# One more expert by seven products, a second buffer pair for the weight sums, and work moved from VectorE to ScalarE in a fused attention, MoE and MLP kernel

## The chip, the cores and the metric

The kernel runs as one program on one core of a Trainium2 chip. A core has TensorE (PE in the rows, its weight loads PEld), VectorE (DVE), ScalarE (ACT), GpSimd (POOL) and SyncE (SP, which here only issues DMAs). The metric is the device time of one execution in microseconds. Everything is float32 at the edges; inside, a float32 operand is split into a rounded high part (type fp32r) and the rest, and one product is made from three TensorE products: high by high, high by rest, rest by high.

## The reference

Three layers follow each other: attention that keeps the 32 largest scores of each row, a mixture of eight experts whose gates are balanced over all tokens, and an MLP with the Mish function whose weights come as float64.

```python
scores = scale * np.matmul(q, k.transpose(0, 1, 3, 2))      # 2 x 8 heads, 576 x 576, head 64
kth = np.partition(scores, -top_k, axis=-1)[..., -top_k:-top_k + 1]
attn = np.matmul(softmax(np.where(scores >= kth, scores, -1e9)), v)
...
P = np.exp(logits - logits.max())                            # 1152 tokens x 8 experts
for _ in range(8):
    P /= P.sum(1, keepdims=True) + 1e-09
    P /= P.sum(0, keepdims=True) + 1e-09
    P *= N / E
for e in range(E):
    out += P[:, e:e + 1] * (np.maximum(x @ w1[e], 0.0) @ w2[e])   # 512 -> 1024 -> 512
...
h = x @ w_in                                                 # 512 -> 2048
return (h * np.tanh(log1p(exp(h)))) @ w_out                  # 2048 -> 512
```

## The kernel before, in words

The 1152 tokens are nine tiles of 128 rows, in three chunks: tiles 0 and 1, tiles 2 and 3, tiles 4 to 8. While VectorE still searches the attention of later tiles for their 32 largest scores, TensorE already runs the experts on the chunks whose attention is done. The gates need all tokens, so the expert outputs of the first two chunks ("spilled" rows, 32 blocks of 128 x 512) go to DRAM as they are. The third chunk (tag c2) starts when attention has ended; from then on its outputs, and the spilled ones that are read back, are multiplied by the gate and added into one accumulator `acc` for each tile. Last comes the MLP in two passes, d0 over tiles 0 to 3 and d1 over tiles 4 to 8.

Weights come in pieces of 128 hidden columns: 128 x 512 of the first layer and 128 x 512 of the second, eight pieces for an expert. In a **plain** piece (`ffn_pass`) the two halves are fetched (`wraw0`, `wraw1`), ScalarE rounds each to its high part (`wh`, line 535), GpSimd or VectorE subtracts for the rest (`wl`, line 536), TensorE makes the first layer (`h`, line 787, 24 products over 640 token columns), ScalarE the high part of the ReLU (`hh`, line 618), VectorE the rest (`hl`, line 619), and two pieces later TensorE the second layer (`y`, line 664, 15 products of 512 columns for five tiles).

In a **pair** (`pair_pass`) two pieces are taken together as a 2 x 2 block product by seven products instead of eight (line 696), each of six TensorE instructions. The seven left sides are made from the two raw weight halves `ra` and `rb` in `load_pair`: the blocks 11 and 12 as they are, the sums s1 to s4 by four GpSimd instructions (lines 557 to 560), and 22. Rounding and subtracting then give `wh` and `wl` of four groups, named 11 (11 and 12), s2 (s2 and s3), s1 (s1 and 22) and s4. The right sides t1 to t4 are sums of token blocks: GpSimd makes those of chunk c2, VectorE those of d0 and d1 (`steps`, lines 595 to 605; "lefts" in the code). TensorE's order in a pair is 11, 12, s2, s3, s1, 22, s4; between them stand the second layers of earlier pieces in halves ("carried", two tiles early, the others late). ScalarE copies partial sums out of PSUM: `p1`, `u2`, `u3` (line 708); VectorE adds them to later ones (`c`, line 714). The bank that holds s3's sum is written again by product 22, so TensorE can go on there only when `u3` is out.

The raw tiles of `ra` and `rb` share three buffers (`wraw0`), each group of `wh` and `wl` has one of four. Experts 0 to 6 of chunk c2 are plain (`PLAIN = 7`), expert 7, d0 and d1 go in pairs.

Beside the products of chunk c2 two other streams are dealt out piece by piece (`pace`): the 32 spilled rows, read back and combined by VectorE (`combine`, lines 806 and 808, 128 x 512 each), and the 32 conversions of the float64 MLP weights (`double_to_float`, lines 929 to 944): a DMA of both words (`cx`), the square of the upper word by ScalarE (`cd`, line 935), six VectorE instructions (lines 936, 939 to 943), a DMA to DRAM. `pace` allows the row n - 10 and the conversion 0.74 (n - 11) + 1 to begin after VectorE's `hl` of piece n. Finished tiles of `acc` are turned by TensorE (`x2t`, line 967, in the PSUM bank "misc" that the pairs also use for product 12) to become the MLP's input.

Engines run their instructions in the order in which a scheduler has put them, TensorE's in the order of the code; each waits at the head of its queue for semaphores. `after(a, b)` puts a behind b in the order without a semaphore.

## Time and profile before

| | us |
|---|---|
| device time, median of 3 runs | 1205.79 |
| lowest and highest of the 3 | 1204.71, 1210.03 |
| the profiled execution | 1205.91 |
| its span, first to last instruction | 1204.1 |
| TensorE busy in the span | 1153.7 |
| VectorE busy | 939.9 |
| ScalarE busy | 695.9 |
| GpSimd busy | 661.0 |

The span is the stretch that the trace covers; the profiled execution took 1.8 us more than it. Attention and the first two chunks take the time to about 556 us, the last product of chunk c2 ends at about 1009, the first of d1 starts at about 1090. In the rows, a group is "line engine operation out<-in, partitions x elements", its count, its busy time and mean, and after the second bar how long the engine stood idle before it and for whom.

### The profile page before, as it was taken

To read this page: it belongs to the slowest core of one execution; us is meant where nothing else is said; L and a number is where in the kernel's file an instruction comes from. 1 tells how busy PE (TensorE), PEld (TensorE's weight loads), DVE (VectorE), ACT (ScalarE), POOL (GpSimd) and SP (SyncE) were. 2 spreads that over 40 slices of the span, in tenths; PEclk is the share of its full clock that TensorE was granted. 3 is DMA by queue.
4 is the path that set the end of the run, shared out by engine and by line. 5 is a ranking of instruction groups with operands and counts; after the bars stand their busy time and mean duration, and the time that the engine had idled before them with its cause. 6 is when DMAs were issued, how large, how long until landed. Compare 5 with 4: busy or idle time off the path is not lost.

```text
span 1204.1 us, 21260 instructions
## 1 busy us (share of the span) xinstructions
PE 1153.7 (96%) x7299; PEld 1028.0 (85%) x7299; DVE 939.9 (78%) x1975; ACT 695.9 (58%) x1414; POOL 661.0 (55%) x559
## 2 busy tenths in 40 slices
PE   3778999999999999999999999999999999999998
PEld 2566888998988899898999989989999998888997
DVE  7999999999999999923666888888767556686442
ACT  5877777777778777754223333333343347666653
POOL 6545877878787777752123243333212466777561
PEclk9999999999999999999999999999999999999999
DMA  8357555557565455544225556656543222223211
GB/s 252 115 181 253 182 182 182 178 174 232 168 215 161 160 167 164 185 141 140 88 85 187 184 193 195 206 184 212 175 155 108 77 73 88 97 97 114 91 51 44
DMA packets 105836, 184.68 MB, mean 153 GB/s; under 512 B 14208, under 2 KB 24704, under 8 KB 105728
## 3 DMA queue, kind: packets, MB, share of 16 engines
q1 hardware_dynamic: 104432, 182.15, 47.2%
q8 instruction: 57, 0.93, 0.3%
q10 hardware_dynamic: 1296, 1.18, 0.3%
q14 instruction: 51, 0.42, 0.1%
HBM read 159.43 MB, written 23.86 MB: 152 GB/s over the span
## 4 chain that ended last, share of the span: by engine, by line
PE 82%; DVE 5%; POOL 3%; DMA 2%; ACT 2%; issue 1%; POOLq 0%; DVEq 0%; ACTq 0%; SPq 0%
PE y_c2e L664 17%; PE h_c2e L787 15%; PE h_c1e L787 8%; PE y_c1e L664 8%; PE y_d L664 6%; PE y_c0e L664 6%; PE h_c0e L787 6%; PE h_d L696 5%; PE pv L356 2%; PE tr L333 2%; PE sc L234 2%; PE h_c2e L696 2%; DVE top L262 1%; PE pv L363 1%; DVE w L269 1%
## 5 line engine op out<-in xcount | busy, mean ns | idle before, releaser
L536 POOL TENSOR_TENSOR wl_c2e<-wraw_c2e,wh_c2e 128x512 fp32r<-128x512 f32 x56 | 75.5, 1348 | 261.9 <-ACT wh_c2e L535 261.9
L536 POOL TENSOR_TENSOR wl_c1e<-wraw_c1e,wh_c1e 128x512 fp32r<-128x512 f32 x128 | 171.7, 1353 | 59.8 <-ACT wh_c1e L535 57.4
L536 POOL TENSOR_TENSOR wl_c0e<-wraw_c0e,wh_c0e 128x512 fp32r<-128x512 f32 x112 | 148.3, 1336 | 49.3 <-ACT wh_c0e L535 43.7
L262 DVE MAX8 top<-w 128x8 f32<-128x576 f32 x216 | 158.4, 748 | 1.0
L535 ACT ACTIVATE wh_c2e<-wraw_c2e 128x512 fp32r<-128x512 f32 x112 | 70.6, 631 | 149.0 <-PE y_c2e L664 67.3
L787 PE MATMUL h_c2e<-xh,wh_c2e 128*128 128x256 f32 x448 | 138.2, 308 | 1.3 <-DVE hl_c2e L619 1.3
L787 PE MATMUL h_c2e<-xl,wh_c2e 128*128 128x256 f32 x448 | 137.4, 307 | 0.0
L787 PE MATMUL h_c2e<-xh,wl_c2e 128*128 128x256 f32 x448 | 137.4, 307 | 0.0
L619 DVE SCALAR_TENSOR_TENSOR hl_c2e<-h_c2e,hh_c2e 128x256 fp32r<-128x256 f32 (+1 forms) x116 | 56.4, 486 | 69.0 <-ACT hh_c2e L618 68.7
L664 PE MATMUL y_c2e<-wh_c2e,hl_c2e 128*128 128x512 f32 x280 | 110.2, 394 | 0.0
L664 PE MATMUL y_c2e<-wh_c2e,hh_c2e 128*128 128x512 f32 x280 | 110.0, 393 | 0.0
L664 PE MATMUL y_c2e<-wl_c2e,hh_c2e 128*128 128x512 f32 x280 | 109.6, 392 | 0.0
L535 ACT ACTIVATE wh_c1e<-wraw_c1e 128x512 fp32r<-128x512 f32 x128 | 80.5, 629 | 47.1 <-PE y_c1e L664 22.1
L269 DVE MATCH_REPLACE8 w<-top,w 128x576 f32<-128x576 f32 x144 | 106.5, 740 | 0.0
L535 ACT ACTIVATE wh_c0e<-wraw_c0e 128x512 fp32r<-128x512 f32 x112 | 70.3, 629 | 43.9 <-PE y_c0e L664 17.6
L787 PEld LDWEIGHTS h_c2e<-xh,wh_c2e 128*128 128x128 f32 x448 | 84.2, 188 | 4.3 <-DVE hl_c2e L619 2.3
L234 PE MATMUL sc<-ks,q 128*128 128x288 f32 x320 | 65.5, 336 | 23.1 <-POOL ks L166 6.1
L787 PEld LDWEIGHTS h_c2e<-xl,wh_c2e 128*128 128x128 f32 x448 | 84.3, 188 | 2.0
L787 PEld LDWEIGHTS h_c2e<-xh,wl_c2e 128*128 128x128 f32 x448 | 84.2, 188 | 0.0
L234 PEld LDWEIGHTS sc<-ks,q 128*128 128x128 f32 x320 | 52.7, 209 | 33.7 <-POOL ks L166 9.9
L787 PE MATMUL h_c1e<-xh,wh_c1e 128*128 128x256 f32 (+1 forms) x256 | 76.4, 298 | 0.0
L787 PE MATMUL h_c1e<-xh,wl_c1e 128*128 128x256 f32 (+1 forms) x256 | 73.3, 286 | 0.0
(540 smaller groups left out, 3622.8 us busy)
## 6 DMA issues: line engine op xcount, KB each, us to landing
wraw_c1e<-in_wst_dram SPq DMA_DIRECT2D x128, 256.0 KB, 2.9
wraw_c0e<-in_wst_dram SPq DMA_DIRECT2D x112, 256.0 KB, 3.0
wraw_c2e<-in_wst_dram SPq DMA_DIRECT2D x112, 256.0 KB, 3.1
cx<-in_w_dram SPq DMA_DIRECT2D x32, 512.0 KB, 3.9
yd<-ysp SPq DMA_DIRECT2D x32, 256.0 KB, 3.6
yb<-yd SPq DMA_DIRECT2D x32, 256.0 KB, 3.4
w<-cb SPq DMA_DIRECT2D x32, 256.0 KB, 3.3
kraw<-in_kT_dram SPq DMA_DIRECT2D x17, 288.0 KB, 3.0
```

The lines of the kernel that those rows point to most:

```text
L234: nc.tensor.matmul(halves[half], q[:, h % HG, :], ks[b, h][:, half * HS : (half + 1) * HS], start=(i == 0), stop=(i == len(terms) - 1),)
L262: top8 = nc.vector.max(g, src)
L269: nc.vector.match_replace(w, g, src, NEG)
L333: nc.tensor.transpose(tr[:, c, :], em[:, j * D + c * P :][:, :P], ident)
L356: nc.tensor.matmul(pv[i * D : (i + 1) * D, pair, c0:c1], vmain[b, pair][:, i, c, :], live["at", i][:, c, c0:c1], start=(c == 0), stop=False,)
L363: nc.tensor.matmul(pv[:, pair, c0:c1], vtail[b, pair], at2[:, c0:c1], start=False, stop=True)
L535: nc.scalar.activation(hi, raw, AF.Copy)
L536: eng.tensor_sub(lo, raw, hi)
L619: live["hl"] = nc.vector.scalar_tensor_tensor(l, ps, 0.0, h, op0=ALU.max, op1=ALU.subtract)
L664: nc.tensor.matmul(y, h[:, j * P : (j + 1) * P], w, start=(start and k == 0), stop=(stop and k == len(products) - 1))
L696: nc.tensor.matmul(bank, a[:, cols], b[:, c, :], start=(start and c + k == 0), stop=(c == 1 and k == 2), skip_group_check=not start,)
L787: nc.tensor.matmul(ps, w[:, c * P : (c + 1) * P], x[:, c, c0 : c0 + m], start=(k == 0), stop=(k == 3 * NC - 1),)
```

## The change

Seven edits are made together. (1) `PLAIN = 6`: experts 6 and 7 of chunk c2 both go in pairs. (2) The conversion's last VectorE instruction, which multiplied by a mask made from ScalarE's square, is gone; ScalarE now makes the absolute value, a first VectorE instruction raises it to 2^-15, and the shift reads that packed result in place of every second word of `cx`. The count stays six. `DOUBLES = 0.87` lets them follow each other faster. (3) A spilled row is scaled by ScalarE, paced behind ScalarE's `hh`, and VectorE only adds; the first row of a tile is written by ScalarE alone. (4) In d0 and d1 `rb` has two buffers of its own (`wrawb`). (5) GpSimd's first three sums stand ahead of the rest of group 11 in the code. (6) The rounding of group s2 is put behind the `u3` of the pair before. (7) The tiles 4 to 8 are turned at other places of d0. `LEFT_FROM = 100` is never reached, so VectorE's t sums of d0 are dealt out in the pairs of experts 6 and 7 alone.

```diff
-TINY2 = ((1 + 1 / 16) * 2.0**-15) ** 2
+TINY = 2.0**-15
...
-PLAIN = 7
-TURN_FROM, LEFT_FROM = 90, 49
-DOUBLES, LEFT_RATE, SUMS = 0.74, (1.5, 0.4), (10, 1.0)
+PLAIN = 6
+TURN_FROM, LEFT_FROM = 90, 100
+DOUBLES, LEFT_RATE, SUMS = 0.87, (1.5, 0.4), (10, 1.0)
...
-    def fetch_raw(a, tag, p):
-        raw = wp.tile([P, DM], F32, tag=f"wraw{a}", name=f"wraw{a}_{tag}", bufs=3)
+    def fetch_raw(a, tag, p, own=False):
+        if own and "x2q" in live:
+            raw = live["x2q"].tile([P, DM], F32, tag="wrawb", name=f"wrawb_{tag}", bufs=2)
+        else:
+            raw = wp.tile([P, DM], F32, tag=f"wraw{a}", name=f"wraw{a}_{tag}", bufs=3)
...
-        nc.scalar.activation(hi, raw, AF.Copy)
+        live["rounded"] = nc.scalar.activation(hi, raw, AF.Copy)
...
-        ra, rb = (fetch_raw(0, f"{tag}{k}", p) for k, p in (("a", pa), ("b", pb)))
+        ra, rb = fetch_raw(0, f"{tag}a", pa), fetch_raw(0, f"{tag}b", pb, True)
...
-        two(("11", "12"), ra)
         nc.gpsimd.tensor_sub(s[:, tail], ra[:, lead], rb[:, lead])
         nc.gpsimd.tensor_add(rb[:, lead], rb[:, lead], rb[:, tail])
         nc.gpsimd.tensor_sub(s[:, lead], rb[:, tail], s[:, tail])
+        two(("11", "12"), ra)
         nc.gpsimd.tensor_sub(ra[:, tail], ra[:, tail], s[:, lead])
         two(("s2", "s3"), s)
+        if "u3" in live:
+            after(live["rounded"], live["u3"])
...
-        sq = cp.tile([P, 512], F32, tag="cd", name=f"cd_{name}")
-        nc.scalar.activation(sq, top.bitcast(F32), AF.Square)
-        begin = nc.vector.tensor_scalar(p2, top, 3, 0x3FFFFFFF, op0=ALU.logical_shift_left, op1=ALU.bitwise_and)
+        m = cp.tile([P, 512], F32, tag="cd", name=f"cd_{name}")
+        nc.scalar.activation(m, top.bitcast(F32), AF.Abs)
+        begin = nc.vector.tensor_scalar(m, m, TINY, None, op0=ALU.max)
...
+        nc.vector.tensor_scalar(
+            p2, m.bitcast(U32), 3, 0x3FFFFFFF, op0=ALU.logical_shift_left, op1=ALU.bitwise_and
+        )
...
-        nc.vector.scalar_tensor_tensor(b, sq, TINY2, b, op0=ALU.is_ge, op1=ALU.mult)
...
-                after(inst, live["hl"])
+                after(inst, live["hi" if kind == "rows" else "hl"])
...
-                paced["rows"].append(combine(t, e, y))
+                begun = t in acc
+                if not begun:
+                    acc[t] = accb.tile([P, DM], F32, tag=f"acc{t}", name=f"acc_{t}")
+                dst = y if begun else acc[t]
+                paced["rows"].append(nc.scalar.activation(dst, y, AF.Copy, scale=gate[:, t, e : e + 1]))
+                if begun:
+                    nc.vector.tensor_add(acc[t], acc[t], y)
...
-            if i >= NPIECE2 // 2 + 2 and i % 2 == 0:
+            if i > NPIECE2 // 2 + 2 and i % 2 and i % 8 != 1:
```

The order of the instructions moves at three places that the prediction speaks of. The first is ScalarE in d0, from `u2` and `u3` of pair 3 to the groups of pair 4 (`wh_d_4_s` are the groups s2 and s1, `wh_d_4b` is a second layer's). Before:

```order
L708 ACTIVATE u_d_3_13274<-h_d_3_0_13239 128x256
L535 ACTIVATE wh_d_4b<-wraw_d_4b 128x512
L535 ACTIVATE wh_d_4_s_13349<-ws_d_4_13340 128x512
L708 ACTIVATE u_d_3_13288<-h_d_3_0_13239 128x256
L648 ACTIVATE mg_d_7_256_13298<-c_d_3_True_13296 128x256
L649 ACTIVATE hh_d_7_13237<-mg_d_7_256_13298 128x256
L535 ACTIVATE wh_d_4_s_13353<-wraw_d_4b 128x512
```

and in the change:

```order
L713 ACTIVATE u_d_3_13374<-h_d_3_0_13339 128x256
L538 ACTIVATE wh_d_4b<-wraw_d_4b 128x512
L713 ACTIVATE u_d_3_13388<-h_d_3_0_13339 128x256
L538 ACTIVATE wh_d_4_s_13449<-ws_d_4_13440 128x512
L653 ACTIVATE mg_d_7_256_13398<-c_d_3_True_13396 128x256
L654 ACTIVATE hh_d_7_13337<-mg_d_7_256_13398 128x256
L538 ACTIVATE wh_d_4_s_13453<-wrawb_d_4b 128x512
```

The rounding of s2 from `ws_d_4` stood ahead of `u3` (the second `u_d_3`); it stands behind it now.

The second place is GpSimd in d0, around the first sum of pair 5 (`ws_d_5` from its two raw tiles). Before:

```order
L536 TENSOR_TENSOR wl_d_4_s_13350<-ws_d_4_13340,wh_d_4_s_13349 128x512
L536 TENSOR_TENSOR wl_d_4_s_13354<-wraw_d_4b,wh_d_4_s_13353 128x512
L536 TENSOR_TENSOR wl_d_4_s_13358<-wraw_d_4a,wh_d_4_s_13357 128x256
L557 TENSOR_TENSOR ws_d_5_13478<-wraw_d_5a,wraw_d_5b 128x256
L536 TENSOR_TENSOR wl_d_5_11_13480<-wraw_d_5a,wh_d_5_11_13479 128x512
L558 TENSOR_TENSOR wraw_d_5b<-wraw_d_5b 128x256
L559 TENSOR_TENSOR ws_d_5_13478<-wraw_d_5b,ws_d_5_13478 128x256
L560 TENSOR_TENSOR wraw_d_5a<-wraw_d_5a,ws_d_5_13478 128x256
L536 TENSOR_TENSOR wl_d_5_s_13488<-ws_d_5_13478,wh_d_5_s_13487 128x512
```

and in the change:

```order
L539 TENSOR_TENSOR wl_d_4_11_13445<-wraw_d_4a,wh_d_4_11_13444 128x512
L559 TENSOR_TENSOR ws_d_5_13578<-wraw_d_5a,wrawb_d_5b 128x256
L563 TENSOR_TENSOR wraw_d_4a<-wraw_d_4a,ws_d_4_13440 128x256
L560 TENSOR_TENSOR wrawb_d_5b<-wrawb_d_5b 128x256
L561 TENSOR_TENSOR ws_d_5_13578<-wrawb_d_5b,ws_d_5_13578 128x256
L539 TENSOR_TENSOR wl_d_4_s_13450<-ws_d_4_13440,wh_d_4_s_13449 128x512
L539 TENSOR_TENSOR wl_d_4_s_13454<-wrawb_d_4b,wh_d_4_s_13453 128x512
L539 TENSOR_TENSOR wl_d_4_s_13458<-wraw_d_4a,wh_d_4_s_13457 128x256
```

The sums of pair 5 stood behind all four groups of pair 4, since `wraw_d_5b` takes the buffer that pair 4 gives up last; they stand between its first and its second group now, and read `wrawb_d_5b`.

The third place is TensorE at the turning of tile 2 in chunk c2's expert 6. Before, between a plain first layer and a second layer:

```order
L787 MATMUL h_c2e_0_256_11640<-xl_4303,wh_c2e_0_11613 128x384
L787 MATMUL h_c2e_0_256_11640<-xh_4302,wl_c2e_0_11614 128x384
L967 MATMUL x2t_11655<-ident,acc_8679 128x128 x4
L664 MATMUL y_c2e_4_11277<-wh_c2e_6_11482,hh_c2e_6_11486 128x512
L664 MATMUL y_c2e_4_11277<-wl_c2e_6_11483,hh_c2e_6_11486 128x512
```

and in the change, right behind product 12 (`hs_c2e_0`, in the bank "misc"):

```order
L701 MATMUL hs_c2e_0_11690<-xl_4303,wh_c2e_0_11_11647 128x320
L701 MATMUL hs_c2e_0_11690<-xh_4302,wl_c2e_0_11_11648 128x320
L974 MATMUL x2t_11701<-ident,acc_8692 128x128 x4
L669 MATMUL y_c2e_4_11305<-wh_c2e_6_11510,hh_c2e_6_11514 128x512
L669 MATMUL y_c2e_4_11305<-wl_c2e_6_11511,hh_c2e_6_11514 128x512
```

Tile 2 is turned in the bank that product 12 has just been written to, where before it followed a product in another bank. In d0, where before one of the five turnings (tile 7) stood right behind a product 12, none does in the change.

## Rows read from the trace of the kernel before

**Rows 1.** Page, busy time and share of the span by engine.

```profile
PE 1153.7 (96%) x7299; PEld 1028.0 (85%) x7299; DVE 939.9 (78%) x1975; ACT 695.9 (58%) x1414; POOL 661.0 (55%) x559
```

**Rows 2.** Waits of PE from 540 us on: total us, times, longest us.

```profile
PE h_d L696 <- ACT u_d L708: 3.0, 5, 0.8
PE h_c2e L787 <- DVE hl_c2e L619: 1.3, 2, 0.9
PE x2t L967 <- DVE c_d_False L714: 0.8, 1, 0.8
```

**Rows 3.** Chain that ended last, late c2: start us, us, what.

```profile
939.09 3.46 PE h_c2e L787 x24
942.56 3.44 PE y_c2e L664 x15
...
950.01 2.07 PE y_c2e L664 x9
...
989.22 2.08 PE y_c2e L664 x9
```

**Rows 4.** The same chain in d0, one turn and its later repeat.

```profile
1040.98 0.63 ACT wh_d_s L535
1041.62 0.28 ACT u_d L708
...
1045.18 2.50 DMA wraw_d_5b<-w
...
1086.23 0.63 ACT wh_d_s L535
```

**Rows 5.** The same chain at the start of d0, where PE alone stands in it.

```profile
1009.33 1.39 PE h_d L696 x12
...
1011.39 1.37 PE y_d L664 x6
```

**Rows 6.** Waits of POOL, 1005 to 1095 us, one of eight such DMA rows.

```profile
POOL ws_d L557 <- DMA wraw_d_7b<-w: 1.6, 1, 1.6
```

**Rows 7.** Busy us (instructions) in two stretches: PE, PEld, DVE, ACT, POOL; clock, DMA share, GB/s.

```profile
637.00:846.00 209.00, 208.13 (x1174) 188.77 (x1174) 174.65 (x269) 72.79 (x141) 74.99 (x61) 1.00 0.61 194
...
1003.00:1095.00 92.00, 88.24 (x553) 78.04 (x552) 68.14 (x107) 63.03 (x146) 65.06 (x63) 1.00 0.27 92
```

**Rows 8.** The same for VectorE's conversions alone (tile cb), first stretch.

```profile
637.00:846.00 209.00, 96.20 (x132) 1.00 0.61 194
```

**Rows 9.** Groups of instructions, shapes apart: conversions, spilled rows, ScalarE copies.

```profile
L313 ACT ACTIVATE em<-em,r 128x576 f32<-128x576 f32 x72 | 55.2, 771 | 10.4 <-DVE r L308 10.2
...
L808 DVE SCALAR_TENSOR_TENSOR acc<-yb,gate,acc 128x512 f32<-128x512 f32 x28 | 28.7, 1024 | 0.0
...
L942 DVE TENSOR_TENSOR cb<-ca,cb 128x512 f32<-128x512 f32 x32 | 25.9, 810 | 0.2
...
L943 DVE SCALAR_TENSOR_TENSOR cb<-cd,cb 128x512 f32<-128x512 f32 x32 | 24.9, 779 | 0.1
...
L936 DVE TENSOR_SCALAR cb<-cx 128x512 uint32<-128x512 uint32 x32 | 24.2, 755 | 0.0
L935 ACT ACTIVATE cd<-cx 128x512 f32<-128x512 f32 x32 | 21.5, 673 | 63.7 <-DMA cx<-in_w_dram 58.1 <-DVE cb L943 4.0 <-DVE acc L808 1.6
...
L940 DVE TENSOR_SCALAR cb<-ca 128x512 uint32<-128x512 uint32 x32 | 15.5, 484 | 0.9
...
L806 DVE TENSOR_SCALAR acc<-yb,gate 128x512 f32<-128x512 f32 x4 | 3.6, 910 | 0.0
```

**Rows 10.** Tile cb's VectorE instructions: duration ns least, median, most; first and last start.

```profile
L936 DVE TENSOR_SCALAR cb<-cx x32: 409/770/1104, 623.9 to 924.0; 128x512 uint32<-128x512 uint32 x32
...
L940 DVE TENSOR_SCALAR cb<-ca x32: 406/426/1362, 628.1 to 925.7; 128x512 uint32<-128x512 uint32 x32
```

**Rows 11.** ScalarE in order of time: start us, us, idle before it and its releaser.

```profile
692.81 0.66 ACT L935 ACTIVATE cd<-cx 128x512 f32<-128x512 f32 x1 [3.37 <-DMA cx<-in_w_dram]
...
702.87 0.67 ACT L935 ACTIVATE cd<-cx 128x512 f32<-128x512 f32 x1 [4.01 <-DVE cb L943]
```

More of the change, by code (lines that the diff above doesn't have):

```diff
@@ L617, in first @@
             h, l = self.hh[:, c0 : c0 + m], self.hl[:, c0 : c0 + m]
-            nc.scalar.activation(h, ps, AF.Relu)
+            live["hi"] = nc.scalar.activation(h, ps, AF.Relu)
             live["hl"] = nc.vector.scalar_tensor_tensor(l, ps, 0.0, h, op0=ALU.max, op1=ALU.subtract)
@@ L707, in kept @@
                 u = tp.tile([P, m], F32, tag="u", name=f"{name}_{tag}_{g}", bufs=3)
-                nc.scalar.activation(u, bank, AF.Copy)
+                live[name] = nc.scalar.activation(u, bank, AF.Copy)
                 return u
@@ L1034, in attention_moe_moe2 @@
     x2q = pool("x2q")
+    live["x2q"] = x2q
     mp = pool("mp")
```

## The prediction

> **What bounds the kernel now.** I read the page first: TensorE is busy for 1153.7 of 1204.1 us [rows 1], so time can be won in two ways only, by giving it less to do or by taking out its waits. Up to the first conversion at about 624 us [rows 10] all engines keep their order, so attention and the first chunks count with nothing. From 540 us on TensorE's waits are three rows [rows 2]: 3.0 us for ScalarE's `u_d` in d0, 1.3 us for VectorE's `hl` in the plain part of chunk c2, 0.8 us of a turning behind VectorE's `c`. Elsewhere the chain that ended last holds products in regular turns [rows 3]. The reader should see there how regular they are: any price on TensorE is a difference of two turns.
>
> In d0 the same chain leaves TensorE [rows 4]: it runs from a DMA of `rb` through GpSimd's sums to the rounding of group s2 on ScalarE, then to `u_d`, and only then to a product. So d0 keeps the time of this loop, not TensorE's.
>
> **Expert 6 by seven products.** A plain piece costs 3.46 + 3.44 = 6.90 us, two of them 13.80. Expert 7 shows the price of a pair of five tiles: from 950.01 to 989.22 lie three pairs [rows 3], 39.21 / 3 = 13.07 us. Expert 6 has four pairs: 4 x 0.73 = **2.9 us less**, if nothing else binds. GpSimd gets 24 instructions more for it, but it was busy for 36% of the stretch ahead (74.99 of 209 us) [rows 7], and expert 7's pairs run in TensorE's own turns with the same GpSimd work, so this costs nothing. If that cover were gone, a pair could take d0's longer turn; that is a rival.
>
> **The loop in d0.** From 1040.98 to 1086.23 the rounding `wh_d_s` comes four pairs later [rows 4]: 45.25 / 4 = 11.31 us for a pair. What TensorE needs for a pair of four tiles can be read where it alone stands in the chain [rows 5]: seven products of 1.39 / 2 us and four half second layers of 1.37, together 10.35 us. The loop thus costs 0.96 us for a pair, 3.8 in the four, and 0.5 us for the first wait, which lies ahead of them: 4.3 us. The waits as put down, 3.0 us, are the lower bound [rows 2]; five full excesses, 4.8 us, the upper.
>
> Why does it go? The loop is: the last group of a pair frees `ra`'s buffer, SP fetches the next `rb` into it (2.50 us [rows 4], for which GpSimd waits another 1.6 us each time [rows 6]), GpSimd makes the sums, ScalarE rounds s2, and `u3` stands behind that rounding. Edit 4 takes the buffer out of the loop: `wrawb` is given back two pairs earlier. Edit 6 takes `u3` out: it stands ahead of the rounding, so that even a late sum no longer holds a product that is due. Either alone should end most of the wait; both together leave the `wh` and `wl` buffers, which TensorE itself frees, as what is late next. Group 11 is free 1.4 us into a pair of 10.35, so about 9 us lie before its next use, and it needs a rounding of 0.63 us [rows 4] and one of GpSimd's eight instructions of a pair. Can GpSimd keep 10.35? It is busy 65.06 of 92 us [rows 7], which is 8.1 turns of 11.31, so 8.0 us for a pair: yes, with 77%. VectorE's 68.14 us make 8.4 us for a pair, 81%. I take **4.3 us less**. Edit 5 moves `wl` of group 11 behind three sums, some 3 us at 1.0 each, which those 9 us cover.
>
> **The turnings.** One of them stands behind a product 12 in d0 and waits 0.8 us for `c` [rows 2]; it goes. In expert 6 tile 2 is now turned right behind `hs_c2e_0`. Its wait is the same row: the product's end, one VectorE addition, then the bank. Bounds are 0 (VectorE faster than the next instructions) and 1.5 us (two instructions of the last conversion, 0.7 to 0.8 us each [rows 9], still stand ahead). I take the same 0.8 us: together **0**.
>
> **VectorE and ScalarE in chunk c2.** The conversions must be through 6 pieces earlier. In the stretch of 209 us VectorE is busy for 174.65, 96.20 of it in 22 conversions (132 instructions) [rows 7, 8]: 4.37 us each. A conversion loses the masking multiply (0.779) and the strided shift (0.755) and gets two dense one-source instructions, for which the nearest row is L940 with 0.484 [rows 9]: 4.37 - 1.53 + 0.97 = 3.81 us. The least durations of the strided and a dense one are 409 and 406 ns [rows 10], so the packing itself may win nothing and the gain only the 0.3 us between 0.779 and 0.484; that bounds it at 4.1. At 0.87 a piece of 6.90 us the stretch holds 26 of them, 99.1 us. A spilled row costs VectorE an addition instead of a multiply and add: 28 x (1.024 - 0.810), and four first rows of 0.910 go [rows 9]: 9.6 us less. So VectorE has 174.65 - 96.20 + 99.1 - 9.6 = 168 us to do, 80% where it had 84%. ScalarE gets 30 scalings of 0.63 to 0.77 us (the nearest copies, L313 at 576 columns) on top of 72.79: some 94 of 209. Both stay off the path; if not, `hl` comes late and TensorE waits for its bank.
>
> That has happened: [rows 11] show ScalarE held for 3.37 and 4.01 us at the square, in front of `hh`, by a `cx` that had not landed and by the buffer of `cd`; I put the longer of the two `hl` waits, 0.9 us [rows 2], down to such holds. The second cause goes, since `cd` is read by the second instruction now, not by the last. The first stays: 58.1 us of such waiting in all [rows 9], and denser conversions leave fewer pieces to catch up: 13 in 100 hold no conversion, where it was 26. The bounds are a gain of 0.9 us (that wait goes; the other of 0.4 lies ahead of the first conversion) and a loss of 3.6 (0.9 us at each of the four ends of an expert in this stretch). I take **0.5 us more**, nearer to the gain, because the sums on VectorE shrink.
>
> **Sum.** -2.9 - 4.3 + 0 + 0.5 = -6.7 us. The profiled execution took 1205.9 us, which is 0.1 over the median of 1205.8, so both give **1199.2**, 0.55% less. A measurement of this kernel can tell about 0.5%, 6.0 us, from no change, and the forecast lies just past that.
>
> **Rivals.**
>
> *d0 keeps its turns* (0.15). For it: a part of the loop stays, since GpSimd's `wl` still waits for ScalarE's `wh`, whose queue also holds `u3`, so it might close there again. Against it: the order shows the sums of pair 5 between groups of pair 4. Then 4.3 us are missing: 1203.5.
>
> *The dense part of chunk c2 stalls* (0.15). For it: the two holds of [rows 11] came with conversions in consecutive pieces, which is now the rule. Against it: fewer us on VectorE. With the 3.6 us above in place of 0.5: 1202.3.
>
> *VectorE's one-source instructions collide with GpSimd* (0.05), the one that ends on the other side. L940 takes 406 ns at the least and 1362 at the most, with the same shape [rows 10]; a conversion has three of these now instead of two, and GpSimd is busy for 36% of the stretch. If each took the longest, a conversion would cost 3.81 + 3 x (1.362 - 0.484) = 6.44 us, 26 of them 167.5, and VectorE would have 236 us to do in 209; TensorE is held to it by `hl`: 27 us more than forecast, 1226. It decides for slower from the point where VectorE's room, 209 - 168 = 41 us, and the 6.7 us won are used up: 1.84 us more for each conversion. With half of all at the longest it would be 34 us of the 48, which does not reach it; hence the small chance. The Trainium skill's page "SBUF — State Buffer" ("Who interferes with whom") states the mechanism as a lock: a VectorE instruction in a two-port mode and a GpSimd instruction take the shared port pair for the whole instruction, and the other one waits. By that rule the long rows are such meetings, and the trace agrees in so far as one and the same instruction lasts 406 or 1362 ns; how often they meet no row here says.
>
> *The change wins more* (0.10): all five waits go, the full 4.8 us, and the new turning is hidden: -2.9 - 4.8 - 0.8 - 0.9 = -9.4, 1196.5.
>
> The forecast itself has 0.55, with 1197.5 to 1201.5 as its own range (the bounds of d0 and about 1.5 us around the 0.5). For the whole I take 1196.2 to 1204.0, which leaves out 2 in 10: the third rival, part of the others beyond their centres. Faster by over 0.5% needs less than 1199.8: some 0.40 of the 0.55, and the 0.10 of the last case, 0.50. The rest of the forecast and the first two rivals are within 0.5%, 0.45 in all. Slower: 0.05.
>
> **What would show it.** In the profile after, expert 6 should show turns of 13.07 us instead of two pieces of 6.90; d0's products about 10.35 us for a pair, with no `u_d` in TensorE's waits and DMA rows gone from GpSimd's; one wait of a turning for `c`, in chunk c2 now; VectorE's share between 637 and 846 us near 80%. It is wrong if d0 still turns in 11 us, if `hl` waits in chunk c2 add up to more than 3 us, or if new waits stand where expert 6 takes over from plain pieces, which no row of before can show for this place, since there the conversions had ended.

## The result and the profile after

The changed kernel takes **1216.55 us** (median of 6 runs, 1212.67 to 1218.97), the kernel before in the same comparison 1205.99 (6 runs, 1204.71 to 1210.03): a ratio of **1.008, 95% interval 1.0062 to 1.0098**. It is slower by 10.6 us, where the forecast said 1199.2 us and 1196.2 to 1204.0 as its range. The profiled execution took 1218.97 us, with a span of 1217.2; it is the slowest of the six, 2.4 us over their median, so what is read from its trace adds up to somewhat more than 10.6.

The page's busy time by engine, to be held against [rows 1]: TensorE's busy time has risen by 6.5 us although it has 24 matmuls less.

```profile
PE 1160.2 (95%) x7275; PEld 1027.3 (84%) x7275; DVE 946.0 (78%) x1983; ACT 720.0 (59%) x1466; POOL 689.4 (57%) x583
```

TensorE's waits from 540 us on (total, times, longest) answer to [rows 2]:

```profile
PE h_c2e L792 <- DVE hl_c2e L624: 9.1, 21, 1.0
PE hs_d L701 <- DVE x2l L978: 1.0, 1, 1.0
PE x2t L974 <- DVE c_c2e_False L719: 0.7, 1, 0.7
PE y_d L669 <- DVE hl_d L655: 0.6, 2, 0.3
```

The waits for `u_d` are gone and the turning waits once in chunk c2, both as forecast. But the wait for `hl` in the plain part of c2, 1.3 us before, is 9.1 us in 21 places, and that is only what stands ahead of matmuls; a late start also stretches what PE counts as busy. How much it is in all, the stages tell. The first product of one stage to the first of the next, read from each trace: the plain part of c2 with the pairs behind it 441.1 us before and 455.3 after; d0 91.9 and 90.1; d1, up to its last product, 109.8 and 109.9. So chunk c2 has lost 14.2 us although it should have won some, and d0 has won 1.9.

What happens in c2 can be seen in one turn of it. This is the timeline of after (start us, us, engine, line, operation; in brackets the idle time ahead and what ended it):

```profile
782.42 0.66 ACT L940 ACTIVATE cd<-cx 128x512 f32<-128x512 f32 x1 [4.75 <-DMA cx<-in_w_dram]
...
784.84 0.42 DVE L624 SCALAR_TENSOR_TENSOR hl_c2e<-h_c2e,hh_c2e 128x256 fp32r<-128x256 f32 x1
784.95 0.33 SPq L934 DMA_DIRECT2D cx<-in_w_dram  x1
...
787.14 0.45 PE L792 MATMUL h_c2e<-xh,wh_c2e 128*128 128x384 f32 x1 [0.18 <-DVE hl_c2e L624]
...
790.17 0.66 ACT L940 ACTIVATE cd<-cx 128x512 f32<-128x512 f32 x1 [4.79 <-DMA cx<-in_w_dram]
790.74 0.62 ACT L538 ACTIVATE wh_c2e<-wraw_c2e 128x512 fp32r<-128x512 f32 x1
...
791.39 0.69 DVE L539 TENSOR_TENSOR wl_c2e<-wraw_c2e,wh_c2e 128x512 fp32r<-128x512 f32 x1 [1.84 <-ACT wh_c2e L538]
...
792.00 0.68 DVE L949 SCALAR_TENSOR_TENSOR cb<-cx,cb 128x512 f32<-128x512 uint32 x1
...
792.71 0.33 SPq L934 DMA_DIRECT2D cx<-in_w_dram  x1
```

Read it from one fetch of `cx` to the next. SP issues the fetch at 784.95. ScalarE runs out of work at 785.4 and then does nothing until the fetch has landed, 5.2 us after its issue: the magnitude (line 940) stands at the head of its queue, and the roundings `wh` and `hh` stand behind it. Then the chain runs through the magnitude (from 790.17), the rounding `wh` (790.74), VectorE's rest `wl` of that rounding (791.39), and only then the multiply of the low words (line 949, 792.00), the last reader of `cx`. This multiply belongs to the conversion before, whose magnitude ran at 782.42; it gives back the other of the two buffers, and SP fetches into that one at 792.71. The turn is 792.71 - 784.95 = **7.76 us**; a plain piece needs 6.90 [rows 3]. With two buffers of `cx` the loop closes on itself, one conversion for each piece, and this piece is 0.86 us late. The chain that ended last runs through just these steps, from fetch to fetch:

```profile
784.95 5.14 DMA cx<-in_w_dram
...
792.08 0.60 DVE cb L949
...
792.71 5.22 DMA cx<-in_w_dram
```

What holds TensorE is `hl`: `hh` comes late behind the magnitude, and on VectorE `hl` stands behind `wl` and the multiply (784.84, with the `hh` that it reads done at 783.9). ScalarE's wait for `cx` between 637 and 860 us is the figure by which the experiments are held against each other:

```profile
ACT cd L940 <- DMA cx<-in_w_dram: 101.5, 22, 7.6
```

The conversions begin at about 624 us, but pieces are late only from 716 us on, when ScalarE's wait ahead of a magnitude has grown from 1.9 us (at 635) to 4.7 (at 713). The twenty plain pieces from there to 871 us take 7.75 us on the mean (6.91 to 9.41), 17.1 us more than twenty of 6.90. Not every one of them is a turn like the one above: the chain holds eight fetches of `cx` there, and in between transfers of `wraw`, `yb` and `cb`, which SP issues from the same queue. The Trainium skill says on its page "PSUM — Partial Sum Buffer" ("Engine vs sequencer instructions") that the queues of ScalarE, VectorE and GpSimd are strict first in, first out. The trace agrees: none of ScalarE's roundings passed the magnitude in the 4.79 us ahead of 790.17.

In the same stretch as [rows 7] VectorE is busy for 163.02 of 209 us, 78%, where it was 84% before. It isn't full. The rows show after in this stretch and in d0:

```profile
637.00:846.00 209.00, 200.96 (x1097) 177.16 (x1096) 163.02 (x264) 80.82 (x160) 70.32 (x56) 1.00 0.60 192
1013.00:1103.00 90.00, 88.16 (x555) 77.78 (x554) 70.48 (x105) 64.04 (x147) 67.81 (x64) 1.00 0.28 94
```

### The profile page after: what moved, and what is told of

Read it like the earlier page. It is cut to its first block, busy times and chain, and to the rows that moved or that the text cites. A ratio compares the mean times of both kernels' runs of the same rounds, so it can differ in the third digit from the quotient of the medians.

```text
span 1217.2 us, 21352 instructions
## 1 busy us (share of the span) xinstructions
PE 1160.2 (95%) x7275; PEld 1027.3 (84%) x7275; DVE 946.0 (78%) x1983; ACT 720.0 (59%) x1466; POOL 689.4 (57%) x583
## 4 chain that ended last, share of the span: by engine, by line
PE 76%; DVE 10%; DMA 8%; ACT 3%; issue 2%; POOL 1%; SPq 0%; ACTq 0%; POOLq 0%; DVEq 0%
PE y_c2e L669 12%; PE h_c2e L792 9%; PE h_c1e L792 8%; PE y_c1e L669 8%; PE y_d L669 8%; PE y_c0e L669 6%; PE h_c0e L792 6%; PE h_d L701 6%; DMA cx<-in_w_dram 4%; PE h_c2e L701 3%; PE pv L356 2%; PE sc L234 2%; DVE top L262 2%; PE tr L333 2%; DMA kraw<-in_kT_dram 2%
## 5 line engine op out<-in xcount | busy, mean ns | idle before, releaser
L792 PE MATMUL h_c2e<-xh,wh_c2e 128*128 128x384 f32 (+1 forms) x384 | 121.7, 317 | 9.5 <-DVE hl_c2e L624 9.1
L792 PE MATMUL h_c2e<-xl,wh_c2e 128*128 128x384 f32 (+1 forms) x384 | 118.2, 308 | 0.0
L792 PE MATMUL h_c2e<-xh,wl_c2e 128*128 128x384 f32 (+1 forms) x384 | 118.1, 308 | 0.0
L269 DVE MATCH_REPLACE8 w<-top,w 128x576 f32<-128x576 f32 x144 | 106.4, 740 | 0.0
L538 ACT ACTIVATE wh_c2e<-wraw_c2e 128x512 fp32r<-128x512 f32 x96 | 60.1, 626 | 70.4 <-PE y_c2e L669 29.5
L940 ACT ACTIVATE cd<-cx 128x512 f32<-128x512 f32 x32 | 21.4, 669 | 129.1 <-DMA cx<-in_w_dram 119.3
L669 PE MATMUL y_c2e<-wh_c2e,hh_c2e 128*128 128x512 f32 x240 | 94.6, 394 | 0.0
L669 PE MATMUL y_c2e<-wl_c2e,hh_c2e 128*128 128x512 f32 x240 | 94.2, 392 | 0.0
L669 PE MATMUL y_c2e<-wh_c2e,hl_c2e 128*128 128x512 f32 x240 | 94.2, 392 | 0.0
L792 PEld LDWEIGHTS h_c2e<-xh,wh_c2e 128*128 128x128 f32 x384 | 72.1, 188 | 19.4 <-DVE hl_c2e L624 18.2
L655 DVE TENSOR_TENSOR hl_d<-mg_d,hh_d 128x256 fp32r<-128x256 f32 (+1 forms) x64 | 51.6, 815 | 33.8 <-ACT hh_d L654 33.8
```

The source lines that it names most:

```text
L269: nc.vector.match_replace(w, g, src, NEG)
L538: live["rounded"] = nc.scalar.activation(hi, raw, AF.Copy)
L655: follow(LEFT_RATE[1], nc.vector.tensor_sub(l, g, h))
L669: nc.tensor.matmul(y, h[:, j * P : (j + 1) * P], w, start=(start and k == 0), stop=(stop and k == len(products) - 1))
L792: nc.tensor.matmul(ps, w[:, c * P : (c + 1) * P], x[:, c, c0 : c0 + m], start=(k == 0), stop=(k == 3 * NC - 1),)
```

## The experiments

The theory (A) is the loop above. Its rivals: VectorE is too slow for 0.87 conversions a piece (B); the row scalings on ScalarE make the first layer's roundings late (C). Twelve kernels were run. All ratios are to the kernel before on the same chip, whose medians there were 1207.0 to 1207.6 us.

### A third buffer of cx, and the magnitude held back

```diff
-        x = cp.tile([P, 512, 2], U32, tag="cx", name=f"cx_{name}")
+        x = cp.tile([P, 512, 2], U32, tag="cx", name=f"cx_{name}", bufs=3)
...
-        a = cp.tile([P, 512], U32, tag="ca", name=f"ca_{name}")
+        a = m.bitcast(U32)
```

> The changed kernel with three buffers for the doubles that a conversion reads (cx) instead of two; to make room, the combined bits are written over the magnitudes (one tile less). Theory A, a closed loop: fetch of cx (5.2 us) - ScalarE's magnitude, which stands waiting at the head of its queue - rounding of a weight - VectorE's low part of it - the instruction that frees the other cx - next fetch, 7.76 us for a piece that needs 6.90. A third buffer lets the fetch start a piece earlier: ScalarE's wait for cx between 637 and 860 us falls from 101.5 to under 20 us, TensorE's wait for hl from 9.1 to under 2, and the kernel takes 1199 to 1203 us. Rival B, VectorE is too slow for 0.87 conversions a piece (its instructions lengthen beside GpSimd): the fetch changes nothing, 1214 to 1219. Rival C, the row scalings on ScalarE delay the first layer's roundings: 1212 to 1219 too.

Measured (e1_cx3): 1201.93 us, ratio 0.9959 (0.9946 to 0.9972), and the plain part of c2 takes 331.8 us where after takes 348.9. ScalarE's row for `cx` is gone from its waits between 637 and 860 us; it waits 31.0 us for the buffer of `cd` in its place, which holds nothing up (TensorE waits for `hl` once in all of c2, 0.7 us at 569 us).

In the second kernel (`abs` is dealt out with `doubles`, behind ScalarE's `hh` instead of VectorE's `hl`):

```diff
-        nc.scalar.activation(m, top.bitcast(F32), AF.Abs)
+        paced["abs"].append(nc.scalar.activation(m, top.bitcast(F32), AF.Abs))
...
-                after(inst, live["hi" if kind == "rows" else "hl"])
+                after(inst, live["hl" if kind == "doubles" else "hi"])
```

> The changed kernel with ScalarE's magnitude held back: it stands behind the rounding of the first layer in the piece in which its conversion begins on VectorE, no longer some 5 us ahead of it. Two cx buffers as before. Theory A: when ScalarE reaches it, the doubles have landed, nothing waits behind it, and the loop is open: 1199 to 1204 us, ScalarE's wait for cx under 20 us. Rival B (VectorE too slow) and rival C (row scalings): 1214 to 1220, or longer, since VectorE then waits for the magnitude.

Measured (e2_abs_late): 1200.82 us, ratio 0.9949 (0.9932 to 0.9966). The plain part of c2 takes 330.7 us, so the loop cost 18.2 us in the trace of after: the 17.1 above, and 1.1 us in the fifteen pieces ahead of 716 us, which take 6.97 us there without a wait and 6.90 here; for that no run has a cause. TensorE's waits from 540 us on in this kernel: the `hl` of chunk c2 is gone, the other three rows are those of after.

```profile
PE hs_d L701 <- DVE x2l L978: 1.0, 1, 1.0
PE x2t L974 <- DVE c_c2e_False L719: 0.7, 1, 0.7
PE y_d L669 <- DVE hl_d L655: 0.6, 2, 0.3
```

Both edits leave the amount of work on VectorE and ScalarE as it is, and both bring the same. Rival B falls with that: in the stretch of [rows 7] VectorE now does 175.91 us of work in 209, more than in after, and TensorE is busy for all 209.

```profile
637.00:846.00 209.00, 209.00 (x1183) 190.10 (x1182) 175.91 (x292) 93.97 (x177) 74.24 (x62) 1.00 0.66 211
```

### The rows on VectorE again

```diff
-                paced["rows"].append(nc.scalar.activation(dst, y, AF.Copy, scale=gate[:, t, e : e + 1]))
-                if begun:
-                    nc.vector.tensor_add(acc[t], acc[t], y)
+                paced["rows"].append(combine(t, e, y))
```

> The changed kernel with the spilled rows combined by VectorE's one instruction, as before the change; ScalarE scales no rows. Theory A: the scalings are no part of the loop of cx, so the loop keeps its 7.7 us a piece: 1213 to 1220 us, with VectorE 4 us busier. Rival C (30 scalings of 0.72 us on ScalarE make the first layer's roundings late): 1199 to 1205. Rival B (VectorE too slow): 1218 to 1224, since VectorE gets 27 x 0.16 = 4.3 us more and TensorE waits for it.

Measured (e3_rows_dve): 1218.18 us, ratio 1.0092 (1.0077 to 1.0108). ScalarE waits for `cx` for 108.4 us between 637 and 860, no less than with the rows on ScalarE. Rival C is out. The time alone would also fit rival B, which has fallen with e2.

### Conversions less dense

```diff
-DOUBLES, LEFT_RATE, SUMS = 0.87, (1.5, 0.4), (10, 1.0)
+DOUBLES, LEFT_RATE, SUMS = 0.74, (1.5, 0.4), (10, 1.0)
```

> The changed kernel with conversions in 74 of 100 pieces, as before the change, in place of 87; the last four are then not paced. Theory A: a piece in four without a conversion gives 6.90 us in which the loop, 0.86 us late for each piece with one, catches up: most of the 16 us go, 1201 to 1206 us, with ScalarE still waiting 40 to 60 us for cx. Rival B (VectorE's work per piece): much the same, 1201 to 1206, but VectorE's instructions then get shorter. Rival C (row scalings): 1213 to 1218, for they stay.

Measured (e4_dens74): 1216.3 us, ratio 1.0076 (1.0049 to 1.0104). Theories A and B are missed by 10 us, and the number lies in the range put down for rival C. It isn't C, as e3 shows: the loss has moved. The plain part of c2 takes 337.2 us, 11.7 less than in after (and 6.5 more than in e2: the loop still holds in runs of consecutive pieces), and the pairs behind it take 117.6 where after has 106.4. The last conversions now run beside expert 6, and there TensorE waits once for 3.2 us at `hl` and for some 1 to 2 us each at a turning and at second layers. So 0.74 is too slow for six plain experts, and density alone doesn't tell the theories apart.

### The old conversion at the new density

```diff
-        nc.scalar.activation(m, top.bitcast(F32), AF.Abs)
-        begin = nc.vector.tensor_scalar(m, m, TINY, None, op0=ALU.max)
+        nc.scalar.activation(sq, top.bitcast(F32), AF.Square)
+        begin = nc.vector.tensor_scalar(p2, top, 3, 0x3FFFFFFF, op0=ALU.logical_shift_left, op1=ALU.bitwise_and)
...
         nc.vector.tensor_add(b, a.bitcast(F32), b)
+        nc.vector.scalar_tensor_tensor(b, sq, TINY2, b, op0=ALU.is_ge, op1=ALU.mult)
```

> The changed kernel with the conversion of before (ScalarE squares, VectorE masks with the square at the end; four of six VectorE instructions shorter by nothing), at 87 conversions in 100 pieces. It tells whether the new conversion or its density closes the loop. Theory A1, density: an instruction of ScalarE that waits for cx holds the queue whichever it is, and two buffers of cx cannot be refetched within 6.90 us: 8 to 16 us slower than the kernel before. Theory A2, the new conversion: it needs ScalarE's result first, where the old one needs it last, so only the new one is tied to ScalarE's queue: 3 to 7 us faster than the kernel before, ScalarE's wait for cx between 637 and 860 us near 50 us.

Measured (e6_conv_old87): 1200.53 us, ratio 0.9938 (0.9925 to 0.9951), with the plain part of c2 at 331.0 us and ScalarE waiting for `cx` for 35.5 us:

```profile
ACT cd L940 <- DMA cx<-in_w_dram: 35.5, 27, 2.8
```

So density alone isn't the cause: six VectorE instructions of the old kind fit as well (VectorE 181.29 of 209 us, TensorE still busy for all of them). The rewritten conversion bought no time that these runs show: with the loop open the new one gives ratios of 0.9959 and 0.9949. The time speaks for A2 as put down, but VectorE's timeline of this kernel shows another reason:

```profile
716.86 0.69 DVE L946 SCALAR_TENSOR_TENSOR cb<-cx,cb 128x512 f32<-128x512 uint32 x1
717.47 0.69 DVE L539 TENSOR_TENSOR wl_c2e<-wraw_c2e,wh_c2e 128x512 fp32r<-128x512 f32 x1
```

Here the multiply that gives `cx` back is the fourth instruction of a conversion, and it stands ahead of `wl`. In the new conversion it is the fifth, and by that one place it has come behind `wl`, which waits for ScalarE:

```profile
719.94 0.43 DVE L948 TENSOR_SCALAR cb<-ca 128x512 uint32<-128x512 uint32 x1
721.15 0.69 DVE L539 TENSOR_TENSOR wl_c2e<-wraw_c2e,wh_c2e 128x512 fp32r<-128x512 f32 x1 [0.78 <-ACT wh_c2e L538]
721.76 0.69 DVE L949 SCALAR_TENSOR_TENSOR cb<-cx,cb 128x512 f32<-128x512 uint32 x1
```

### Two VectorE instructions exchanged

The changed kernel, with `wl` put behind the multiply that frees `cx`:

```diff
+            if q % 8 != 4 and q - 2 in freed:
+                after(live["low part"], freed[q - 2])
```

> The changed kernel with one pair of VectorE's instructions exchanged in most pieces: the conversion's multiply of the low words, which gives back cx, stands ahead of the low half of the second weight (wl), which waits for ScalarE. The magnitude stays where it is. In the changed kernel wl stands first, so the fetch hangs on ScalarE's queue; with the old conversion (e6) the multiply is one instruction earlier and stands ahead. Theory A3, that order closes the loop: 4 to 8 us faster than the kernel before, ScalarE's wait for cx between 637 and 860 us from 101.5 down to 30 to 60 us. Rival A2, it is enough that the magnitude stands waiting in ScalarE's queue while the conversion needs it first: 6 to 12 us slower than the kernel before.

Measured (e10_low_first): 1202.2 us, ratio 0.9957 (0.994 to 0.9974). The magnitude still stands in ScalarE's queue ahead of its time, for 49.0 us between 637 and 860 where after has 101.5:

```profile
ACT cd L946 <- DMA cx<-in_w_dram: 49.0, 25, 3.2
```

TensorE has no wait for `hl` in c2 any more, and the plain part takes 330.8 us. A3 holds, A2 falls: a held ScalarE alone costs nothing here, since the fetch no longer hangs on it.

### Expert 6, and d0 alone

The kernel with the magnitude held back (e2), expert 6 plain again:

```diff
-PLAIN = 6
+PLAIN = 7
```

> The kernel with the magnitude held back (e2_abs_late) and expert 6 plain again (7 plain experts; the left operands' pace as before). It prices the step for expert 6: seven products save 4 x 0.73 = 2.9 us, and the turning in expert 6 costs 0.8: e2's distance to the kernel before (6.8 us) shrinks by 2.1, to 4.7 us. Rival: the conversions leave the plain pieces more room, and the plain version is as fast as e2, or expert 6 costs more than its turns: 6 to 8 us under the kernel before.

Measured (e8_plain7): 1203.14 us, ratio 0.996 (0.9948 to 0.9973), 3.9 us under the kernel before, where e2 is 6.8 under it: a difference of 2.9 us, where the expectation had 2.1 and the rival none or the other sign. The traces tell why. Expert 6 takes 56.1 us here and 54.1 in e2, so its pairs win 2.0, as expected. The rest is expert 7: one of its pairs takes 13.8 us here, with a second layer that waits 0.5 us for `hl`, and 13.1 in e2. By stages c2 takes 439.8 us here and 437.0 in e2.

Then the edits made for d0, on the kernel before (`fetch_raw` with its own buffer, the order of the sums, `u3`, the turning places):

```diff
-        ra, rb = (fetch_raw(0, f"{tag}{k}", p) for k, p in (("a", pa), ("b", pb)))
+        ra, rb = fetch_raw(0, f"{tag}a", pa), fetch_raw(0, f"{tag}b", pb, True)
...
+        if "u3" in live:
+            after(live["rounded"], live["u3"])
...
-            if i >= NPIECE2 // 2 + 2 and i % 2 == 0:
+            if i > NPIECE2 // 2 + 2 and i % 2 and i % 8 != 1:
```

> The kernel before with the edits of stage d0 alone: the buffer of its own for rb, the sums ahead, u3 ahead of the rounding of s2, the other turning places. My step: 4.3 us less by the loop, 0.8 less at the turning, and 1.2 more where the first product into the misc bank now waits for the low half of a turned tile: 3.9 us less than the kernel before in all (3.0 to 5.0). Rival: without the edits in chunk c2, the loop of d0 goes over to another wait and at most 1.5 us are won.

Measured (e7_d0_only): 1205.51 us, ratio 0.9985 (0.9975 to 0.9995), so 1.5 us less. That is the rival's number, but not its mechanism: d0 takes 89.0 us where before takes 91.9, 2.9 less, and four of its pairs turn in 10.4 us each. In the profile c2 takes 1.6 us more (389.8 and 53.0 us for its two parts, before 388.8 and 52.3), with 2.4 us of waiting for `hl` where [rows 2] have 1.3. In the plain part a mishap that before has once, at 702 us, comes twice, at 703 and 815 us; none of these edits touches plain pieces, and why it comes twice no run settles. In the pairs the edits aren't of d0 alone: `load_pair` serves expert 7 of c2 too, so the order of the sums and the place of the rounding change there as well, and one pair takes 13.8 us, with a wait for `hl`.

### The turning places, and which edit of d0 works

e2 with other places for the turnings:

```diff
-        if i >= TURN_FROM and i % 2 == 0:
+        if i in (90, 92, 95, 97):
...
-            if i > NPIECE2 // 2 + 2 and i % 2 and i % 8 != 1:
+            if i >= NPIECE2 // 2 + 2 and i % 2 == 0 and i % 8:
```

> e2_abs_late with other turning places: in expert 6 the third and fourth tile are turned behind the half second layers, not behind hs; in d0 behind s2, s1 and 22 again, leaving out only the place behind product 12. The traces of after and of e2 show 0.8 us at the first place and 1.2 us at the second (the first product into the misc bank waits for the turned tile's low half): 2.0 us less than e2, 8.8 us under the kernel before. Rival: each stall only moves to the next wait on the same bank, and e9 equals e2 within 0.7 us.

Measured (e9_turns): 1204.93 us, ratio 0.9981 (0.9971 to 0.9991): 2.1 us under the kernel before where e2 is 6.8 under it, so both expectations are missed. d0 did win, 87.8 us where e2 has 90.2, but the pairs of c2 take 112.2 where e2 has 106.4. The list of places was at fault. The t sums of d0 ("lefts" in the code, left operands in the expectations) are dealt out to VectorE from a list that is filled one step after the last turning. With four steps that happened only behind the loop, nothing paced them, and VectorE took them up at once, in front of `hl` in expert 6:

```profile
902.43 1.52 DVE L608 TENSOR_TENSOR x<-x 128x256 f32<-128x256 f32 x1
903.87 0.74 DVE L813 SCALAR_TENSOR_TENSOR acc<-y_c2e,gate,acc 128x512 f32<-128x512 f32 x1
904.53 0.99 DVE L624 SCALAR_TENSOR_TENSOR hl_c2e<-c_c2e_True,hh_c2e 128x320 fp32r<-128x320 f32 x1
905.44 0.41 DVE L610 TENSOR_TENSOR t_d<-x,t_d 128x256 fp32r<-128x256 f32 x1
...
906.97 0.48 DVE L624 SCALAR_TENSOR_TENSOR hl_c2e<-h_c2e,hh_c2e 128x320 fp32r<-128x320 f32 x1
```

One step more mends it:

```diff
-        if i in (90, 92, 95, 97):
+        if i in (90, 92, 95, 97, 99):
```

> e9_turns with a fifth step, at which the list of d0's left operands is made while the pacing still runs; in e9 this list was made after the loop, its VectorE work was not paced and stood in front of hl in expert 6 (3.5 us of waiting there, and TensorE's granted clock at 0.76 for the 7 us behind it). Theory: expert 6 then has neither this stall nor the turning's 0.8 us, d0 takes 87.8 us as in e9 where e2 has 90.2: 3 us under e2, 9 to 10 us under the kernel before. Rival: the turning places themselves load VectorE in expert 6, and 3 us or more are lost there again: 2 to 6 us under the kernel before.

Measured (e11_turns2): **1197.65 us, ratio 0.9914 (0.99 to 0.9928)**, 9.65 us under the kernel before, faster than both kernels of this case. The pairs of c2 take 105.5 us, d0 87.6. TensorE's only wait from 540 us on, and the page's row by engine:

```profile
PE h_d L701 <- ACT p_d L713: 0.2, 1, 0.2
```

```profile
PE 1147.7 (96%) x7275; PEld 1024.2 (86%) x7275; DVE 942.2 (79%) x1983; ACT 724.3 (61%) x1466; POOL 685.3 (57%) x583
```

On this version the two edits of d0 were undone one at a time.

```diff
-        ra, rb = fetch_raw(0, f"{tag}a", pa), fetch_raw(0, f"{tag}b", pb, True)
+        ra, rb = fetch_raw(0, f"{tag}a", pa), fetch_raw(0, f"{tag}b", pb)
```

> e11_turns2 without the buffer of its own for rb (rb shares the three buffers of the first weights again, as before the change); u3 stays ahead of the rounding of s2. My step said that either edit alone ends most of the wait in d0: within 1 us of e11. Rival: only both together open the loop, since GpSimd's sums still wait for rb's transfer: d0 turns in 11 us again and it is 3 to 5 us behind e11.

Measured (e12_no_own): 1199.35 us, ratio 0.9928 (0.9914 to 0.9943), 1.7 us behind e11; d0 takes 89.7 us, and TensorE waits 1.7 us for `hl` there. The 1.7 us lie between what the theory and the rival had put down. GpSimd waits for `rb` in eight rows again, as before the change; with the buffer it does so in three.

```diff
-        if "u3" in live:
-            after(live["rounded"], live["u3"])
```

> e11_turns2 without the order of u3 ahead of the rounding of s2; rb keeps its own buffer. My step said that either edit alone ends most of the wait in d0: within 1 us of e11. Rival: ScalarE's rounding still waits for the last of GpSimd's sums with u3 behind it: d0 turns in 11 us and it is 3 to 5 us behind e11.

Measured (e13_no_u3): 1197.62 us, ratio 0.9913 (0.9897 to 0.9929), d0 87.6 us: no different from e11. So the buffer does all of it without the order of `u3`. That order without the buffer takes 2.2 of the 4.3 us between before and e11; the new turning places are in this too. The new order of GpSimd's sums stands in both kernels; no run undoes it.

## Why the prediction was wrong

**The step that failed: VectorE and ScalarE in chunk c2.** It took +0.5 us, between -0.9 and +3.6; the loop costs 18.2 us (348.9 - 330.7), 16.9 if the 1.3 of old `hl` waits that went are set against it. The step summed busy time and asked whether two engines stay under 209 us. They do, and that was not the question: VectorE's share near 80%, put down as a sign of being right, came out at 78% in a kernel that had lost 10 us. The step saw ScalarE held for `cx` [rows 9, 11], knew that one of two causes stayed, and priced that one as single mishaps: 0.9 us at the four ends of an expert. It didn't follow the hold around. The sentence that `cd` is now read by the second instruction was right, but the same edit put one instruction more ahead of the last reader of `cx`, and that one place moved the reader behind `wl`.

That much could be read before the run: the order of the changed kernel has `wl` ahead of the multiply, and the trace of before gives the parts, 0.67 us for ScalarE's instruction [rows 9], 0.63 for a rounding [rows 4], and on the mean 0.72 for `wl` and 0.74 for the multiply in the first stretch of [rows 7], some 2.7 in all. The loop passes 6.90 us as soon as a fetch takes more than 4.2. The page's DMA part gives a median of 3.9 for before and 5.0 for after, so the working would have ended 0.3 us under the edge: no proof of a loss, but no cover either. Why the fetch takes 5.0 us in after and 4.2 to 4.7 in the kernels of equal density with the loop open (e6, e1, e10, e2, e11), no run settles. The second rival, a stall in the dense part, had the place and the sign, with a fifth of the size, because it borrowed this price.

The price was misread in part, too. The 0.9 us wait of [rows 2] ends at 702.24, and the hold of 4.01 us in [rows 11] at 702.87: that hold is no cause of it. The other hold, up to 692.81, is one, but through VectorE, which begins late behind it (694.40) and then works without a pause, with two instructions at about twice their usual 0.7 us, beside GpSimd:

```profile
694.40 0.56 DVE L619 SCALAR_TENSOR_TENSOR hl_c2e<-h_c2e,hh_c2e 128x384 fp32r<-128x384 f32 x1 [3.96 <-ACT hh_c2e L618]
...
698.77 1.80 DVE L536 TENSOR_TENSOR wl_c2e<-wraw_c2e,wh_c2e 128x512 fp32r<-128x512 f32 x1
700.48 1.37 DVE L942 TENSOR_TENSOR cb<-ca,cb 128x512 f32<-128x512 f32 x1
```

The `hl` for which TensorE waited starts only at 701.77, though its `hh` was done at 696.4. So ScalarE's holds already reached TensorE by way of VectorE's queue.

The price of the conversion was off as well, with no effect: 3.81 us were forecast, 3.90 stand in e2's groups between 637 and 846 us; but the old kind at the new density takes 4.04 there, not 4.37, so the gain is 0.14 us and not 0.56. A row's addition takes 0.89 us there, not 0.81. The stretch needs 175.91 us of VectorE, not 168.

**Expert 6** held: its pairs turn in 13.1 us, as the chain of after shows for `hs` (three turns from the first row to the last, 39.24 us); the first turn, with the turnings in it, takes 14.8. Won were 2.0 us (56.1 in e8, 54.1 in e2), and forecast were 2.9 less the turning's 0.8.

```profile
922.30 0.88 PE hs_c2e L701 x6
...
935.40 0.88 PE hs_c2e L701 x6
...
961.54 0.88 PE hs_c2e L701 x6
```

**The loop in d0** held in the mechanism: TensorE's waits for `u_d` are gone, and from product 12 to product 12 four pairs in the middle of d0 take 11.2 us each before, 10.6 in after and 10.4 in e11, where 11.31 and 10.35 were worked out. That d0 goes from 91.9 to 87.6 us in e11, by just the 4.3 forecast, is in part luck: the 0.8 us wait of the old turning behind product 12, which the forecast took as a term of its own, is in these 4.3, so 5.1 were forecast for d0 in all. No run opens the loop with the old turning places, so the two can't be parted. That either edit alone would end most of it was half right: the buffer does, `u3` doesn't. GpSimd's waits for `rb` were to go; three of eight rows stay, at no cost to TensorE (in before they range from 0.6 to 1.7 us; the 1.6 "each time" is one of them). In after only 1.9 of the 4.3 could be seen, because of the next step.

**The turnings**, taken as 0 with bounds of 0 and 1.5, cost more. The place in expert 6 costs 0.9 (106.4 us for the pairs in e2, 105.5 in e11; 0.7 of it stands as a wait), near the 0.8 forecast. In d0 the wait behind product 12 went, and another came that the step hadn't looked for: the place behind the carried second layer stands so near to the next product 12 that this waits in the bank "misc" for VectorE's `x2l`, 1.0 us by the waits and 1.2 by that pair's length against e11. And two second layers wait for `hl` behind VectorE's t sums of d1, 0.3 us each by the waits; their pairs are 0.8 and 0.3 us longer than in e11. The chain of after shows the first two of these three, where [rows 4] had the DMA and ScalarE:

```profile
1037.44 0.61 DVE x2l L978
...
1038.18 0.94 PE hs_d L701 x6
...
1070.69 1.02 DVE x L608
...
1073.62 0.89 DVE hl_d L655
1074.52 0.04 issue
1074.56 1.20 PE y_d L669 x4
```

With the other places all are gone (e11). That the second kind hung on when the list of t sums is filled is argued from the code, not shown by a run.

**Sum.** Against before, after's stages give +18.2 (loop), -2.0 (expert 6 with its turning), -2.1 (the other plain pieces: 386.8 us in e8, 388.8 before; 1.3 of it are the old `hl` waits, 0.7 a piece at the start of c2) and -1.9 (d0), some 12.3 us; 0.5 is that c2 begins later, 0.3 lies in d1 and behind it, and the two spans differ by 13.1. The third rival, VectorE's one-source instructions against GpSimd, gave 1226 and has the sign of the result but not its mechanism: such meetings are frequent (below), but the dense shift of line 944 has a median of 414 ns in after, the maximum of line 941 624, which in e2 is 914 on the mean between 637 and 846 us, at no cost to TensorE; and the 1240 ns of line 950 went with the loop (below).

## What to carry to other kernels

When an edit adds an instruction ahead of the one that frees a DMA buffer, follow the buffer around once: fetch, every queue in which its readers stand, the instruction that frees it, next fetch; if that sum passes the time of the piece that it serves, every such piece pays, however idle the engines are, and a piece without a fetch gives nothing back to an engine that is full. An instruction that waits for a transfer belongs in an in-order queue as late as its consumer allows, and a reader that frees a buffer ahead of instructions that wait for other engines; here either was a change of order alone, and won the same as a third buffer. And when a place in an order is moved, ask what else was counted from that place.

## What the runs showed of the hardware

**One VectorE instruction lasts twice as long beside GpSimd.** The last sum of a conversion (line 950, two inputs in SBUF) in after and in e2, duration least, median, most:

```profile
L950 DVE TENSOR_TENSOR cb<-ca,cb x32: 674/1240/1462, 630.4 to 901.4; 128x512 f32<-128x512 f32 x32
```

```profile
L950 DVE TENSOR_TENSOR cb<-ca,cb x32: 677/680/1321, 629.7 to 882.2; 128x512 f32<-128x512 f32 x32
```

In after 20 of the 32 ran beside a GpSimd instruction for at least 30% of their time and have a median of 1441 ns; the other 12 have 680. In the turn shown above it stands beside GpSimd's `wl`, which the same held rounding had released:

```profile
784.46 1.61 POOL L539 TENSOR_TENSOR wl_c2e<-wraw_c2e,wh_c2e 128x512 fp32r<-128x512 f32 x1 [4.83 <-ACT wh_c2e L538]
...
785.18 1.44 DVE L950 TENSOR_TENSOR cb<-ca,cb 128x512 f32<-128x512 f32 x1
```

The Trainium skill's page "SBUF — State Buffer" ("Who interferes with whom") says that a VectorE instruction with two SBUF inputs contends with a GpSimd instruction that reads SBUF; the trace agrees. It isn't what closed the loop: e2 and e10 run the same instruction, and without the loop the two mostly miss each other. The one-source instruction of line 941 shows the like: in e2 the 4 of its 32 that ran apart from GpSimd took 408 to 417 ns, the 28 beside it 668 to 1102; in after it is 408 to 417 against 619 to 1532, with one exception of 423.

**TensorE's clock fell behind two long stalls.** In e9 TensorE waited 3.5 us for `hl`, up to 907.5 us. The windows ahead of it, around it and behind it (span, busy us of each engine, granted clock third from last):

```profile
895.00:903.00 8.00, 8.00 (x45) 7.03 (x44) 5.92 (x11) 3.85 (x9) 2.07 (x2) 1.00 0.10 34
903.00:907.00 4.00, 0.98 (x7) 0.72 (x5) 4.00 (x8) 1.05 (x2) 1.60 (x3) 1.00 0.44 115
907.00:914.00 7.00, 6.32 (x26) 5.36 (x26) 7.00 (x15) 2.08 (x5) 4.16 (x5) 0.76 0.14 48
```

Between 909.83 and 911.54 the second layer's matmuls follow each other at 0.43 us, where they do at 0.23 at full clock: the lower of the two levels, 1.2 GHz. In e4 it happened once more: TensorE was busy for 1.80 us of the five from 913 us and for 3.50 of the five from 918, and the granted clock was 0.76 between 923 and 930 us. In after, where the stalls last up to 1.0 us each, it is 1.00 between 637 and 860 us.
